# The second weight matrix of a dense layer: turned on TensorE, or read and converted a second time

## The chip, the cores and the metric

One core of one Trainium2 chip runs the whole program. The metric is the device time of one execution in microseconds (us). The kernel before took 642.76 us, the median of three runs (639.36, 642.76 and 643.01).

## The reference: what is computed

Three stages follow one another.

```
attention, 4 batches x 12 heads, 448 tokens, head width 64:
  s = 30 * tanh(q k^T / 8 / 30);  x = softmax(s) v            -> x: 1792 tokens x 768
dense layer:  r = relu(x @ w_in);  g = s*r*r + b;  y = g @ w_out   w_in 768x2048, w_out 2048x768
soft mixture on y:  logits = y @ phi (32 slots)
  d = softmax over tokens, c = softmax over slots
  slot_in = d^T y;  h = relu(slot_in[e] @ w1[e]);  out = c @ (h @ w2[e])     8 experts, 4 slots each
```

The inputs are float32, but `w_in` and `w_out` arrive as float64 and have to be made into float32 on the chip. The program never forms y. It uses `w_out @ phi` (for the logits), and applies `w_out` once to the 32 rows of slot inputs, near the end. So it needs `w_out` with the 2048 hidden units on the partitions in the tail, and with the 768 output columns on the partitions for the product with `phi`.

## The kernel before

**Blocks.** One batch is one block (448 tokens), 0 to 3. `hidden` makes relu(x w_in)^2 of a block in 16 slices `fc` of 128 hidden units, each with 18 products `hp` (L527): six 128-row pieces of x times three products, since each fp32 factor is split in two parts, hi and lo. The attention of block b+1 is laid between the products of block b, so TensorE does both in blocks 0 to 2. Block 3 has no attention beside it. The tail applies `w_out`, `w1` and `w2` to the slots.

**Attention.** Heads go in fours (`Q`, twelve in all, three to a block). `scores` (L137, L134) or, from the seventh four on, `visit` (L165, L155) makes a piece of 128 keys: products `sc` of 64 rows, two heads side by side in the array, three products per factor split. `weighted` (L243) makes `U`: products with 32 columns, four heads side by side. `sums` (L226) makes the softmax sums the same way, and `post` (L564) the logits `L`.

**Weights of a slice.** A slice's `w_in` arrives in `wr`; `w_split` makes each of its two halves into hi (ScalarE, L511) and lo (VectorE, L512) in `ws`. Three halves are held: two belong to the slice in work, one to the next. `wr` has three buffers.

**Conversion.** `convert` takes float64 pieces of 128 x 768 (768 KB, buffer `raw`, three of them). A piece costs one pass on ScalarE (L372) and three on VectorE (L377, L401, L405). The 16 pieces of `w_in` go into `wr` and, for blocks 1 to 3, to DRAM (`wsc`), from where L498 reads them again. `w_out` comes in transposed form (`w_outT`): 8 pairs of pieces into a buffer `o`, of which there is one. For a pair, `down` multiplies by `phi` (`pp`, L457), `fold` adds up (`pf`, L465), and three calls of `wturn` turn it by 128 x 128 transposes on TensorE (`tw`, L475, four a call), copy the result from PSUM (ScalarE, L477) and store it to DRAM (`osc`, L478). The tail reads `osc` in the wanted form. Turns, transposes of r (`tp`, L550), sums, `pp` and `pf` share one PSUM bank until block 3.

**Order.** Engines run their instructions in a fixed order each. A scheduler makes this order when the program is built: it takes what is ready by its own estimates, the earliest traced first, unless a priority or an issue-after edge says otherwise. `convert` is a generator that is advanced once per third of a slice in blocks 0 and 1 (`block`, L802), and when a slice of `w_in` or a part of `w_out @ phi` is needed. All loads and stores of weights are issued on one queue, SP's, in order. The program holds two copies of the body, chosen by a flag at run time; cap is 30 here, so the first runs.

Of the kernel before, what the change touches and what calls it, by code (L numbers as in the profile page):

```python
# [7 lines left out]
F32 = mybir.dt.float32  # L8
# [9 lines left out]
P = 128  # L18
B, H, S, D = 4, 12, 448, 64
# [4 lines left out]
DM = H * D  # L24
KC = DM // P
FF = 2048
FC = FF // P
# [6 lines left out]
KF = S // P  # L34
# [6 lines left out]
LAST = 3  # L41
CASTS = 8
LEAD = 10
WIDE = 6
VISITS = (4, 7, 10, 13)
U = 256
CU = 768
HOLD = 2
XPOS = (1, 4, 7, 10, 13, 15, 15, 15)
POSTS = [[(), (), (0,), (1,)], [(-2,), (-1,), (0, 1), (2,)], [(-1,), (0,), (1,), (2,)], [(-1,), (0,), (1,), (2,)]]  # L50
OUT_GROUPS = [(0, 4), (4, 6)]
# [8 lines left out]
class Body:  # L60
    def __init__(self, nc, tc, io, consts, general, f64, wsc, osc):
        self.nc, self.tc, self.io, self.c, self.general = nc, tc, io, consts, general
        self.f64, self.wsc, self.osc = f64, wsc, osc
        self.ws, self.wr = {}, {}
        self.x = {}
        self.qk = {}
        self.r2 = {}
        self.e = {}
        self.v = {}
        self.nslot = 0  # L70
        self.later, self.wide, self.nsplit = [], False, 0
        self.nx = 0
        self.mark = None
        self.raws = 3

    def bank(self, name):
        return self.pst[0].tile([P, 512], F32, tag="T", bufs=self.pst[1], name=name)
# [48 lines left out]
    def scores(self, p, c):  # L126

        nc = self.nc
        Q, j = divmod(p, 2)
        qh, ql, kh, kl = self.qk[p]  # L130
        sc = (self.ps2 if self.ps2 is not None and j else self.psa).tile([P, 2, 512], F32, tag="sc", bufs=1, name="sc")
        for n, (k, q) in enumerate(((kh, qh), (kh, ql), (kl, qh))):
            if c == KF:
                nc.tensor.matmul(sc[:, 0, :S], k[:, KF * P:], q, start=(n == 0), stop=(n == 2))  # L134
            for i in range(2) if c < KF else ():
                r = slice(64 * i, 64 * i + 64)
                nc.tensor.matmul(sc[:, i, :S], k[r, c * P:(c + 1) * P], q[r, :], start=(n == 0), stop=(n == 2))  # L137
        if j == 0:
            self.e.setdefault(Q, []).append(self.ap.tile([P, 4 if c < KF else 2, S], F32, tag="e", bufs=4 if self.general else 3, name="e"))
        if c < KF:  # L140
            nc.scalar.activation(self.e[Q][c][:, 2 * j:2 * j + 2, :], sc[:, :, :S], AF.Tanh, scale=self.c["tsc"])  # L141
        else:
            nc.scalar.activation(self.e[Q][c][:, j, :], sc[:, 0, :S], AF.Tanh, scale=self.c["tsc"])
        if c == NCH - 1:
            del self.qk[p]

    def visit(self, Q, c):

        nc = self.nc
        t = [self.qk[2 * Q + j] for j in range(2)]  # L150
        if c == KF:
            sc = self.psa.tile([P, 2, 512], F32, tag="sc", bufs=1, name="sc")
            for j, (qh, ql, kh, kl) in enumerate(t):
                for n, (k, q) in enumerate(((kh, qh), (kh, ql), (kl, qh))):
                    nc.tensor.matmul(sc[:, j, :S], k[:, KF * P:], q, start=(n == 0), stop=(n == 2))  # L155
            self.e[Q].append(self.ap.tile([P, 2, S], F32, tag="er", bufs=1, name="er"))
            nc.scalar.activation(self.e[Q][c], sc[:, :, :S], AF.Tanh, scale=self.c["tsc"])
            del self.qk[2 * Q], self.qk[2 * Q + 1]
            return
        sc = [self.psa.tile([P, 2, 512], F32, tag=n, bufs=1, name="sc") for n in ("sc", "U")]  # L160
        for j, (qh, ql, kh, kl) in enumerate(t):
            for n, (k, q) in enumerate(((kh, qh), (kh, ql), (kl, qh))):
                for i in range(2):
                    r = slice(64 * i, 64 * i + 64)
                    nc.tensor.matmul(sc[j][:, i, :S], k[r, c * P:(c + 1) * P], q[r, :], start=(n == 0), stop=(n == 2))  # L165
        self.e.setdefault(Q, []).append(self.ap.tile([P, 4, S], F32, tag="e", bufs=3, name="e"))
        for j in range(2):
            nc.scalar.activation(self.e[Q][c][:, 2 * j:2 * j + 2, :], sc[j][:, :, :S], AF.Tanh, scale=self.c["tsc"])  # L168
# [65 lines left out]
    def weighted(self, Q, chunks):  # L234

        nc = self.nc
        if chunks[0] == 0:
            self.U = self.psa.tile([P, 2, 512], F32, tag="U", bufs=1, name="U")
        for k in chunks:
            for h in range(2):  # L240
                for i in range(4):
                    d = (i % 2 * KF + k if k < KF else 2 * KF) * D + 32 * h
                    nc.tensor.matmul(self.U[32 * i:32 * i + 32, h, :S], self.v[2 * Q + i // 2][self.rows(i, k), d:d + 32], self.chunk(4 * Q + i, k),  # L243
                                     start=(k == 0), stop=(k == KF))

    def finish(self, Q):

# [176 lines left out]
    def conv_units(self):  # L424


        nc, io, c = self.nc, self.io, self.c
        cur = {}
# [9 lines left out]
        def across(fh, half):  # L438
            if half == 0:
                self.wide = True  # L440
                cur["o", fh] = self.cv.tile([P, KC * U], F32, tag="o", bufs=1, name="o")
            return cur["o", fh][:, half * CU:(half + 1) * CU]

        def proj(fh, half):
            if half == 0:
                return
            o = cur.pop(("o", fh)).rearrange("p (a b) -> p a b", b=U)
            self.later = [lambda: down(fh, o)]
            if self.f64:
                self.later += [lambda th=th: wturn(fh, th, o) for th in range(3)]  # L450
            self.later.insert(2, lambda: fold(fh))

        def down(fh, o):
            pp = self.bank("pp")
            for kc in reversed(range(KC)):
                j = kc % 4
                nc.tensor.matmul(pp[32 * j:32 * j + 32, :U], c["phi"][:, kc, :], o[:, kc, :], start=(kc + 4 >= KC), stop=(kc < 4))  # L457
            nc.scalar.copy(c["tmp"][:, S + U * (fh % 2):S + U * (fh % 2 + 1)], pp[:, :U])
            self.wide = self.f64

        def fold(fh):
            ps = c["tmp"][:, S + U * (fh % 2):S + U * (fh % 2 + 1)]
# [5 lines left out]
            if self.nx == FF // U:  # L468
                self.bias()

        def wturn(fh, th, o):
            tw = self.bank("tw")
            for j in range(2):
                for k in range(2):
                    nc.tensor.transpose(tw[:, (2 * j + k) * P:(2 * j + k + 1) * P], o[:, 2 * th + k, j * P:(j + 1) * P], c["idn"])  # L475
            n = o[:, 2 * th:2 * th + 2, :].rearrange("p a b -> p (a b)")
            nc.scalar.copy(n, tw)  # L477
            nc.sync.dma_start(self.osc[th][:, 2 * U * fh:2 * U * (fh + 1)], n)  # L478
            self.wide = th < 2

        units = []
        for fc in range(FC):
            units.append((io["w_in"][fc], lambda fc=fc: place(fc), lambda o, fc=fc: keep(fc, o), lambda fc=fc: self.nsplit + 3 > fc))
            for fh in range(FF // U):
                if XPOS[fh] == fc:
                    units += [(io["w_outT"][fh, h], lambda fh=fh, h=h: across(fh, h), lambda o, fh=fh, h=h: proj(fh, h), lambda h=h: h or not self.wide) for h in range(2)]
        return units

    def w_need(self, i):
# [228 lines left out]
    def prefetch(self, upto, behind=False):  # L718

        while self.nslot < min(upto, 54):  # L720
            k, h = divmod(self.nslot, 2)
            self.wt[k, h] = self.half(self.nslot)
            src = (self.osc if self.f64 else self.io["w_out"])[k] if k < 3 else self.io["w1"][k - 3] if k < 15 else self.io["w2"][k - 15]
            with self.tc.issue_after(self.mark) if behind else nullcontext():
                self.nc.sync.dma_start(self.wt[k, h], src[:, 2048 * h:2048 * (h + 1)])
            self.nslot += 1
# [59 lines left out]
    def block(self, bi, atn):  # L786
# [5 lines left out]
        for grp in range(4):  # L792
# [6 lines left out]
            for k in range(12):  # L799
                next(h)  # L800
                next(post, None)
                if bi < 2:  # L802
                    next(self.conv, None)
                while done < min(total, (12 * grp + k + 1) * total / (48 - LEAD)):
                    next(atn)
                    done += 1
# [122 lines left out]
def tile_kernel(ctx: ExitStack, tc: tile.TileContext, io):  # L929
# [43 lines left out]
    t("pb", [P, 1])  # L973
    t("ct", [P, NT], F32R)
    f64 = io["w_in"].dtype == I64
    osc = []
    dp = ctx.enter_context(tc.tile_pool(name="dp", bufs=1, space=DRAM))
    wsc = [dp.tile([P, KC * P], F32, name=f"wsc{i}") for i in range(FC)]
    if f64:
        osc = [dp.tile([P, 4096], F32, name=f"osc{i}") for i in range(3)]  # L980
    rv = nc.values_load(flag, min_val=0, max_val=1, skip_runtime_bounds_check_because="a comparison writes 0 or 1")
    with tc.If(rv > 0) as br:
        Body(nc, tc, io, c, False, f64, wsc, osc).run()
# [4 lines left out]
def layouts(inputs):  # L988
# [19 lines left out]
    wi = wi.reshape(NQ, 4, 2, D // 2, FF).transpose(0, 2, 1, 3, 4)  # L1008
    a["w_in"] = cc(wi.reshape(KC, P, FC, P).transpose(2, 1, 0, 3)).reshape(FC, P, KC * P)
    a["w_outT"] = cc(wo.reshape(FF // U, U, 2, KC // 2, P).transpose(0, 2, 4, 3, 1)).reshape(FF // U, 2, P, CU)  # L1010
    if not f64:
        a["w_out"] = cc(wo.reshape(FC, P, 3, U).transpose(2, 1, 0, 3)).reshape(3, P, 4096)
    a["phi"] = cc(inputs["moe2_phi"].reshape(KC, P, NS).transpose(1, 0, 2))
    a["w1"] = cc(inputs["moe2_w1"].reshape(2, 4, KC, P, F2).transpose(0, 2, 3, 1, 4)).reshape(2 * KC, P, 4096)
    a["w2"] = cc(inputs["moe2_w2"].reshape(2, 4, FC2, P, NPC, P).transpose(4, 0, 3, 2, 1, 5)).reshape(2 * NPC, P, 4096)
# [32 lines left out]
```

## Time and profile before

| | |
|---|---|
| runs | 639.36, 642.76, 643.01 us |
| profiled execution | 638.93 us, span of its instructions 637.2 us |
| TensorE (PE) busy, weight loads (PEld) | 593.7 us, 396.3 us |
| VectorE (DVE), ScalarE (ACT) busy | 343.4 us, 402.1 us |
| HBM read, written | 118.49 MB, 18.09 MB |
| first `hp` of blocks 0, 1, 2, 3; last `hp` | 66.5, 196.6, 327.9, 446.6; 523.9 us |

A row of the page or of the trace gives an engine, a line of the kernel, the tile written and the tiles read. A fp32 product that is not split appears as two records, so `U` of a four of heads, one piece of keys, is 16 records. Matmuls overlap: the next starts while one is still under way. So the time that a group takes from TensorE is read from its first start to the first start of the next group, not from the length of its records.

### The profile page before, as it was taken

What the parts mean: (1) busy time and instruction counts of PE and PEld (TensorE: products, weight loads), DVE (VectorE), ACT (ScalarE), POOL (GpSimd) and SP (SyncE); (2) the same over time, 40 slices, a digit from 0 to 9 for tenths busy, and PEclk for the clock granted to TensorE, in tenths of its full rate; (3) what the DMA queues carried; (4) which work ended last, traced back from release to release, by engine and by line L of the source; (5) the groups of instructions that cost most, each with busy time, mean ns of one, the idle gap of its engine ahead of it and who ended that gap; (6) DMA issues with size and microseconds to landing.
All of it is one profiled execution on the core that took longest, in us unless ns stands there. A gap on an engine that the chain in (4) does not pass through costs nothing.

```text
span 637.2 us, 11290 instructions
## 1 busy us (share of the span) xinstructions
PE 593.7 (93%) x4592; PEld 396.3 (62%) x4592; DVE 343.4 (54%) x509; ACT 402.1 (63%) x683; POOL 4.1 (1%) x11
## 2 busy tenths in 40 slices
PE   8898999999999999999999999999999998998672
PEld 5333575746776747567687476768868884346461
DVE  4998899878894482844624825454332224112121
ACT  5887889879867959679569386866645662001010
POOL 1000000000000000000000000000000000000000
PEclk9998999999999999999999999999999999999997
DMA  8843778786685442221421221211968859999998
GB/s 297 290 128 115 269 262 300 252 274 199 235 299 198 136 154 83 87 78 50 141 75 52 84 75 40 72 54 56 394 256 313 315 190 394 421 419 417 419 412 318
DMA packets 39626, 137.38 MB, mean 216 GB/s; under 512 B 4352, under 2 KB 12304, under 8 KB 32656
## 3 DMA queue, kind: packets, MB, share of 16 engines
q1 hardware_dynamic: 39280, 136.07, 59.2%
q8 instruction: 38, 0.62, 0.4%
q0 software_dynamic: 288, 0.53, 0.2%
q14 instruction: 20, 0.16, 0.1%
HBM read 118.49 MB, written 18.09 MB: 214 GB/s over the span
## 4 chain that ended last, share of the span: by engine, by line
PE 65%; DMA 14%; DVE 9%; ACT 8%; issue 3%; SPq 0%; DVEq 0%; ACTq 0%
PE hp L527 32%; DMA wt<-in_w_dram 12%; PE U L243 9%; PE tp L550 4%; PE sc L165 3%; PE pt L640 2%; PE L L564 2%; PE sc L137 2%; PE Sm L226 2%; ACT e L206 2%; ACT e L168 1%; PE tw L475 1%; DVE rec L232 1%; DMA osc<-o 1%; PE pp L457 1%
## 5 line engine op out<-in xcount | busy, mean ns | idle before, releaser
L527 PE MATMUL hp<-x,ws 128*128 128x448 f32 x1152 | 271.4, 376 | 0.0
L527 PEld LDWEIGHTS hp<-x,ws 128*128 128x128 f32 x1152 | 206.4, 188 | 42.2 <-issue 29.4
L512 DVE TENSOR_TENSOR ws<-wr,ws 128x384 fp32r<-128x384 f32 x128 | 70.6, 553 | 123.3 <-ACT ws L511 123.1
L511 ACT CAST ws<-wr 128x384 fp32r<-128x384 f32 x128 | 66.8, 524 | 36.8 <-PE hp L527 36.3
L243 PE MATMUL U<-e,v 128*32 128x448 f32 (+1 forms) x672 | 75.8, 551 | 4.7 <-ACT e L206 3.7
L206 ACT ACTIVATE e<-e,c_acap 128x1792 f32<-128x1792 f32 (+1 forms) x42 | 71.5, 1702 | 0.5
L552 ACT COPY g<-tp 112x256 f32<-112x256 f32 x128 | 43.3, 385 | 12.8 <-PE tp L550 12.0
L243 PEld LDWEIGHTS U<-e,v 128*32 128x32 f32 (+1 forms) x672 | 20.7, 110 | 45.4 <-issue 36.3
L232 DVE RECIPROCAL rec<-rec 128x448 f32<-128x448 f32 x12 | 35.4, 2950 | 18.1 <-ACT rec L231 18.1
L141 ACT ACTIVATE e<-sc,c_tsc 128x896 f32<-128x896 f32 x36 | 35.9, 1008 | 12.9 <-PE sc L137 11.9
L533 ACT ACTIVATE r<-hp 128x448 f32<-128x448 f32 x63 | 34.9, 554 | 9.8 <-PE hp L527 9.8
L550 PE MATMUL tp<-c_cst,r 128*112 128x128 f32 x256 | 39.0, 275 | 1.7 <-ACT g L552 1.4
L897 ACT COPY wt<-op 128x512 f32<-128x512 f32 x12 | 7.0, 586 | 50.6 <-PE op L892 50.6
L168 ACT ACTIVATE e<-sc,c_tsc 128x896 f32<-128x896 f32 x36 | 36.1, 1035 | 4.0 <-PE sc L165 4.0
L534 ACT ACTIVATE r<-r 128x448 f32<-128x448 f32 x63 | 37.6, 596 | 0.4
L912 PE MATMUL so_ps<-wt,free 128*32 128x128 f32 x768 | 26.5, 282 | 10.9 <-DMA wt<-in_w_dram 10.5
L550 PEld LDWEIGHTS tp<-c_cst,r 128*112 128x112 f32 x256 | 29.5, 133 | 11.3 <-ACT g L552 3.8
L215 DVE TENSOR_TENSOR es<-e 128x1792 f32<-128x1792 f32 x12 | 24.3, 2022 | 13.7 <-ACT e L206 13.7
L912 PEld LDWEIGHTS so_ps<-wt,free 128*32 128x32 f32 x768 | 20.8, 113 | 15.2 <-DMA wt<-in_w_dram 12.8
L215 DVE TENSOR_TENSOR es<-es,e 128x1792 f32<-128x1792 f32 x12 | 24.3, 2022 | 9.6 <-ACT e L206 9.6
L231 ACT ACTIVATE rec<-Sm,c_eps 128x448 f32<-128x448 f32 x12 | 7.7, 638 | 28.9 <-PE Sm L226 28.9
L863 PE MATMUL hps<-wt,free 128*32 128x512 f32 x192 | 21.0, 593 | 0.0
(186 smaller groups left out, 705.9 us busy)
## 6 DMA issues: line engine op xcount, KB each, us to landing
wt<-in_w_dram SPq DMA_DIRECT2D x48, 1024.0 KB, 16.5
wr<-wsc SPq DMA_DIRECT2D x48, 384.0 KB, 3.1
raw<-in_w_in_dram SPq DMA_DIRECT2D x16, 768.0 KB, 5.2
raw<-in_w_outT_dram SPq DMA_DIRECT2D x16, 768.0 KB, 5.8
wsc<-wr SPq DMA_DIRECT2D x16, 384.0 KB, 3.0
osc<-o SPq DMA_DIRECT2D x24, 256.0 KB, 2.9
wt<-osc SPq DMA_DIRECT2D x6, 1024.0 KB, 7.0
k<-in_kT_dram SPq DMA_DIRECT2D x22, 256.0 KB, 3.4
```

What stands on the lines that cost most here:

```text
L168: nc.scalar.activation(self.e[Q][c][:, 2 * j:2 * j + 2, :], sc[j][:, :, :S], AF.Tanh, scale=self.c["tsc"])
L206: ins = self.nc.scalar.activation(e, e, AF.Exp, scale=self.c["acap"]).ins
L215: self.nc.vector.tensor_add(es, e[0] if c == 1 else es, e[c])
L232: nc.vector.reciprocal(self.rec, self.rec)
L243: nc.tensor.matmul(self.U[32 * i:32 * i + 32, h, :S], self.v[2 * Q + i // 2][self.rows(i, k), d:d + 32], self.chunk(4 * Q + i, k), start=( ...
L511: self.nc.scalar.copy(hi, u)
L512: self.nc.vector.tensor_sub(lo, u, hi.bitcast(F32))
L527: nc.tensor.matmul(hp[:, :S], ws[kc // 3][:, w, kc % 3, :], x[:, s, kc, :], start=(k == 0), stop=(k == 3 * KC - 1))
L534: self.mark = nc.scalar.activation(r2, r2, AF.Square).ins
L550: self.nc.tensor.transpose(tp[:CP, q * P:(q + 1) * P], r2[:, q * CP:(q + 1) * CP], self.c["idn"])
L552: self.nc.scalar.copy(self.g[q][:CP, :, fc * P:(fc + 1) * P], tp[:CP, 2 * q * P:2 * (q + 1) * P].rearrange("p (a b) -> p a b", b=P))
L912: nc.tensor.matmul(so_ps[32 * e:32 * e + 32, G, :], ht[G][:, f, 32 * e:32 * e + 32], w2[f // 4][:, f % 4, e, :], start=(f == 0), stop=(f = ...
```

## The change

`wturn` is gone: no transposes `tw`, no copies from PSUM, no stores of turned pieces. Instead `w_out` is given to the program a second time, untransposed, in 16 pieces of 768 KB. They are units of the same generator `convert`, behind all others, and they may start when slices 22, 23, 25, 26, 28, ... 44 (of 64, counted over the blocks) have been split: in blocks 1 and 2. Each is stored to `osc` as three runs of 1 KB per partition. The generator is now advanced in all blocks, and holds four turns instead of two before it does `down`. The second part is `together`: the products of a score visit, or of a call of `weighted`, are placed behind their first one with a high priority (for `weighted` from the fourth four of heads on, for scores from the third pair on). In `visit` the hi and lo parts now come in the opposite order.

```diff
+VISIT = 3000
+LAY = (22, 3, 2)
-HOLD = 2
+HOLD = 4
...
+    def together(self, products, near=True):
+
+        if not near:
+            products = [f() for f in products]
+            return
+        first, rest = products[0](), products[1:]
+        with self.tc.issue_after(first.ins), self.tc.high_priority(VISIT):
+            for p in rest:
+                p()
...
+        if p < 2:
+            for f in products:
+                f()
+        else:
+            self.together(products)
...
+        self.together([lambda j=j, n=n, k=k, q=q, i=i, r=r: nc.tensor.matmul(sc[j][:, i, :S], k[r, c * P:(c + 1) * P], q[r, :], start=(n == 0), stop=(n == 2))
+                       for j, (qh, ql, kh, kl) in enumerate(t) for n, (k, q) in enumerate(((kl, qh), (kh, ql), (kh, qh))) for i, r in enumerate(half)])
...
+        self.together(products, Q >= 3)
...
-            self.later = [lambda: down(fh, o)]
-            if self.f64:
-                self.later += [lambda th=th: wturn(fh, th, o) for th in range(3)]
-            self.later.insert(2, lambda: fold(fh))
+            self.later = [lambda: down(fh, o), lambda: fold(fh)]
...
-            self.wide = self.f64
+            self.wide = False
...
-        def wturn(fh, th, o):
-            tw = self.bank("tw")
-            for j in range(2):
-                for k in range(2):
-                    nc.tensor.transpose(tw[:, (2 * j + k) * P:(2 * j + k + 1) * P], o[:, 2 * th + k, j * P:(j + 1) * P], c["idn"])
-            n = o[:, 2 * th:2 * th + 2, :].rearrange("p a b -> p (a b)")
-            nc.scalar.copy(n, tw)
-            nc.sync.dma_start(self.osc[th][:, 2 * U * fh:2 * U * (fh + 1)], n)
-            self.wide = th < 2
+        def lay(fc):
+            if fc % 2 == 0:
+                cur["n"] = self.cv.tile([P, KC * U], F32, tag="o", bufs=1, name="o")
+            return cur["n"][:, fc % 2 * DM:(fc % 2 + 1) * DM]
+
+        def store(fc, o):
+            nc.sync.dma_start(self.osc.rearrange("p (t f d) -> p t f d", t=3, d=U)[:, :, fc, :], o.rearrange("p (t d) -> p t d", d=U))
...
+        a, n, d = LAY
+        for fc in range(FC if self.f64 else 0):
+            units.append((io["w_out"][fc], lambda fc=fc: lay(fc), lambda o, fc=fc: store(fc, o), lambda fc=fc: self.nsplit >= a + fc * n // d))
...
-                if bi < 2:
-                    next(self.conv, None)
+                next(self.conv, None)
...
-        osc = [dp.tile([P, 4096], F32, name=f"osc{i}") for i in range(3)]
+        osc = dp.tile([P, 3 * 4096], F32, name="osc")
```

TensorE's order in block 0, a little past its middle, before: a score visit (three rows `sc`, two products each) and a `U` of 16 products.

```order
L137 MATMUL sc<-qh,kh 128x448 x2
L243 MATMUL U<-e,v 32x448 x5
L137 MATMUL sc<-ql,kh 128x448 x2
L457 MATMUL pp<-o,c_misc 32x256 x6
L137 MATMUL sc<-qh,kl 128x448 x2
L243 MATMUL U<-e,v 32x448 x4
L475 MATMUL tw<-c_cst,o 128x128 x4
L243 MATMUL U<-e,v 32x448 x7
L527 MATMUL hp<-x_398,ws 128x448 x6
```

The same place in the order of the change:

```order
L146 MATMUL sc<-qh,kh 128x448 x2
L146 MATMUL sc<-ql,kh 128x448 x2
L146 MATMUL sc<-qh,kl 128x448 x2
L257 MATMUL U<-e,v 32x448 x16
L238 MATMUL Sm<-es,c_ones 32x448 x4
L541 MATMUL hp<-x_396,ws 128x448 x6
L564 MATMUL tp<-c_cst,r_794 112x128 x4
```

The visit and `U` stand in one piece each and `tw` is gone. Between the first and the last `hp` of the program, runs of `sc` go from 65 (28, 21 and 16 in blocks 0, 1 and 2) to 49 (22, 14, 13), runs of `U` from 17 (10, 3, 4) to 12 (6, 3, 3), and runs of `tw` from 24 (18, 6, 0) to none.

VectorE's order in the second half of block 2, before: the last step of a four of heads (`U` times the reciprocal of the sums, then the lo part of x) and the lo parts of the weights, `ws`.

```order
L255 TENSOR_TENSOR U<-U,rec 128x2x448
L512 TENSOR_TENSOR ws<-wr,ws 128x384
L81 TENSOR_TENSOR x_2321<-U,x_2321 128x896
L512 TENSOR_TENSOR ws<-wr,ws 128x384 x9
L215 TENSOR_TENSOR es<-e 128x1792
```

In the order of the change, the same step and what follows it:

```order
L271 TENSOR_TENSOR U<-U,rec 128x2x448
L526 TENSOR_TENSOR ws<-wr,ws 128x384
L421 SCALAR_TENSOR_TENSOR o<-raw,o 128x768
L93 TENSOR_TENSOR x_2168<-U,x_2168 128x896
L526 TENSOR_TENSOR ws<-wr,ws 128x384 x3
L393 TENSOR_SCALAR o<-o 128x768
L526 TENSOR_TENSOR ws<-wr,ws 128x384
L417 SCALAR_TENSOR_TENSOR o<-raw,o 128x768
L393 TENSOR_SCALAR o<-o 128x768
L421 SCALAR_TENSOR_TENSOR o<-raw,o 128x768
L526 TENSOR_TENSOR ws<-wr,ws 128x384
L417 SCALAR_TENSOR_TENSOR o<-raw,o 128x768
```

Passes of the second conversion (`o`) now stand between the `ws` rows, up to three in a row.

## Rows read from the trace of the kernel before

**Rows 1.** The page, part 1: busy time of each engine and its share.
```profile
PE 593.7 (93%) x4592; PEld 396.3 (62%) x4592; DVE 343.4 (54%) x509; ACT 402.1 (63%) x683; POOL 4.1 (1%) x11
```
**Rows 2.** Busy by stretch: blocks 0 to 3, tail; us, PE, PEld, DVE, ACT, POOL, clock, DMA.
```profile
66.50:196.60 130.10, 128.53 (x825) 85.32 (x824) 112.33 (x141) 107.68 (x176) 0.00 (x0) 1.00 0.77 265
196.60:327.90 131.30, 128.72 (x868) 87.15 (x867) 71.85 (x100) 97.88 (x173) 0.54 (x1) 1.00 0.34 107
327.90:446.60 118.70, 117.74 (x778) 81.67 (x777) 58.07 (x76) 84.59 (x146) 0.00 (x0) 1.00 0.21 63
446.60:524.50 77.90, 77.90 (x448) 64.36 (x447) 22.50 (x49) 45.49 (x108) 0.00 (x0) 1.00 0.77 292
524.50:637.20 112.70, 83.04 (x1264) 51.17 (x1262) 24.67 (x66) 13.80 (x27) 0.54 (x1) 0.94 0.99 400
```
**Rows 3.** PE's waits in block 0: us in total, times, longest.
```profile
PE pp L457 <- DVE o L405: 1.0, 2, 0.8
```
**Rows 4.** PE's waits in block 1.
```profile
PE pp L457 <- DVE o L405: 1.8, 2, 1.4
```
**Rows 5.** Timeline of PE, a turn between other products: start, length, what.
```profile
173.00 0.66 PE L475 MATMUL tw<-c_cst,o 128*128 128x128 f32 x4
173.41 0.85 PE L527 MATMUL hp<-x,ws 128*128 128x448 f32 x3
```
**Rows 6.** Timeline of PE in block 0, a visit and a U in pieces.
```profile
132.44 0.48 PE L137 MATMUL sc<-qh,kh 64*128 64x448 f32 x2
132.85 1.69 PE L243 MATMUL U<-e,v 128*32 128x448 f32 x10
134.47 0.47 PE L137 MATMUL sc<-ql,kh 64*128 64x448 f32 x2
134.87 1.06 PE L457 MATMUL pp<-o,c_misc 128*32 128x256 f32 x12
135.86 0.47 PE L137 MATMUL sc<-qh,kl 64*128 64x448 f32 x2
136.26 1.82 PE L243 MATMUL U<-e,v 128*32 128x448 f32 x8
138.01 0.66 PE L475 MATMUL tw<-c_cst,o 128*128 128x128 f32 x4
138.60 1.70 PE L243 MATMUL U<-e,v 64*32 64x448 f32 x14
140.23 1.48 PE L527 MATMUL hp<-x,ws 128*128 128x448 f32 x6
```
**Rows 7.** Timeline of PE in block 0, a visit and a U in one piece.
```profile
76.09 0.48 PE L137 MATMUL sc<-qh,kh 64*128 64x448 f32 x2
...
76.91 3.21 PE L243 MATMUL U<-e,v 128*32 128x448 f32 x32
80.05 1.27 PE L527 MATMUL hp<-x,ws 128*128 128x448 f32 x5
```
**Rows 8.** DVE and others from 78 to 110 us, columns as in Rows 2.
```profile
78.00:110.00 32.00, 30.87 (x210) 20.40 (x204) 31.14 (x40) 29.20 (x45) 0.00 (x0) 1.00 0.79 282
```
**Rows 9.** Groups by line, whole span: busy us, mean ns, idle before.
```profile
L401 DVE SCALAR_TENSOR_TENSOR o<-raw,o 128x768 int32<-128x768 int32 x16 | 15.1, 951 | 0.1
L405 DVE SCALAR_TENSOR_TENSOR o<-raw,o 128x768 int32<-128x768 int32 x16 | 15.1, 950 | 0.1
L372 ACT ACTIVATE o<-raw 128x768 f32<-128x768 f32 x16 | 14.4, 929 | 1.8 <-DMA osc<-o 1.1 <-DMA raw<-in_w_outT_dram 0.7
L477 ACT COPY o<-tw 128x512 f32<-128x512 f32 x24 | 14.1, 586 | 5.8 <-PE tw L475 5.7
L377 DVE TENSOR_SCALAR o<-o 128x768 int32<-128x768 int32 x16 | 8.8, 554 | 3.2 <-ACT o L372 3.1
```
**Rows 10.** Groups of DVE by line within block 0 alone.
```profile
L405 DVE SCALAR_TENSOR_TENSOR wr<-raw,wr 128x768 int32<-128x768 int32 x13 | 12.3, 950 | 0.1
L405 DVE SCALAR_TENSOR_TENSOR o<-raw,o 128x768 int32<-128x768 int32 x10 | 9.5, 950 | 0.0
```

More of the change, by code (lines that the diff above doesn't have):

```diff
@@ L131, in scores @@
         sc = (self.ps2 if self.ps2 is not None and j else self.psa).tile([P, 2, 512], F32, tag="sc", bufs=1, name="sc")
[L132 to L137, printed above, removed]
+        halves = [(0, slice(0, P))] if c == KF else [(i, slice(64 * i, 64 * i + 64)) for i in range(2)]
+        terms = ((kh, qh), (kh, ql), (kl, qh))
+        products = [lambda n=n, k=k, q=q, i=i, r=r: nc.tensor.matmul(sc[:, i, :S], k[r, c * P:(c + 1) * P], q[r, :], start=(n == 0), stop=(n == 2))
+                    for n, (k, q) in enumerate(terms) for i, r in halves]
+        if p < 2:
[3 more added lines that the diff above has]
+            self.together(products)
         if j == 0:
@@ L152, in visit @@
             sc = self.psa.tile([P, 2, 512], F32, tag="sc", bufs=1, name="sc")
-            for j, (qh, ql, kh, kl) in enumerate(t):
-                for n, (k, q) in enumerate(((kh, qh), (kh, ql), (kl, qh))):
-                    nc.tensor.matmul(sc[:, j, :S], k[:, KF * P:], q, start=(n == 0), stop=(n == 2))
+            self.together([lambda j=j, n=n, k=k, q=q: nc.tensor.matmul(sc[:, j, :S], k[:, KF * P:], q, start=(n == 0), stop=(n == 2))
+                           for j, (qh, ql, kh, kl) in reversed(list(enumerate(t))) for n, (k, q) in enumerate(((kl, qh), (kh, ql), (kh, qh)))])
             self.e[Q].append(self.ap.tile([P, 2, S], F32, tag="er", bufs=1, name="er"))
@@ L160, in visit @@
         sc = [self.psa.tile([P, 2, 512], F32, tag=n, bufs=1, name="sc") for n in ("sc", "U")]
[L161 to L165, printed above, removed]
+        half = [slice(64 * i, 64 * i + 64) for i in range(2)]
+        self.together([lambda j=j, n=n, k=k, q=q, i=i, r=r: nc.tensor.matmul(sc[j][:, i, :S], k[r, c * P:(c + 1) * P], q[r, :], start=(n == 0), stop=(n == 2))
+                       for j, (qh, ql, kh, kl) in enumerate(t) for n, (k, q) in enumerate(((kl, qh), (kh, ql), (kh, qh))) for i, r in enumerate(half)])
         self.e.setdefault(Q, []).append(self.ap.tile([P, 4, S], F32, tag="e", bufs=3, name="e"))
@@ L238, in weighted @@
             self.U = self.psa.tile([P, 2, 512], F32, tag="U", bufs=1, name="U")
-        for k in chunks:
+        order = tuple(chunks)
+        products = []
+        for k in order:
             for h in range(2):
@@ L242, in weighted @@
                     d = (i % 2 * KF + k if k < KF else 2 * KF) * D + 32 * h
-                    nc.tensor.matmul(self.U[32 * i:32 * i + 32, h, :S], self.v[2 * Q + i // 2][self.rows(i, k), d:d + 32], self.chunk(4 * Q + i, k),
-                                     start=(k == 0), stop=(k == KF))
+                    products.append(lambda k=k, h=h, i=i, d=d: nc.tensor.matmul(
+                        self.U[32 * i:32 * i + 32, h, :S], self.v[2 * Q + i // 2][self.rows(i, k), d:d + 32], self.chunk(4 * Q + i, k),
+                        start=(k == 0), stop=(k == KF)))
+        self.together(products, Q >= 3)
     def finish(self, Q):
@@ L722, in prefetch @@
             self.wt[k, h] = self.half(self.nslot)
-            src = (self.osc if self.f64 else self.io["w_out"])[k] if k < 3 else self.io["w1"][k - 3] if k < 15 else self.io["w2"][k - 15]
+            src = (self.osc[:, 4096 * k:4096 * (k + 1)] if self.f64 else self.io["w_out"][k]) if k < 3 else self.io["w1"][k - 3] if k < 15 else self.io["w2"][k - 15]
             with self.tc.issue_after(self.mark) if behind else nullcontext():
@@ L975, in tile_kernel @@
     f64 = io["w_in"].dtype == I64
-    osc = []
+    osc = None
     dp = ctx.enter_context(tc.tile_pool(name="dp", bufs=1, space=DRAM))
@@ L1010, in layouts @@
     a["w_outT"] = cc(wo.reshape(FF // U, U, 2, KC // 2, P).transpose(0, 2, 4, 3, 1)).reshape(FF // U, 2, P, CU)
-    if not f64:
-        a["w_out"] = cc(wo.reshape(FC, P, 3, U).transpose(2, 1, 0, 3)).reshape(3, P, 4096)
+    a["w_out"] = wo.reshape(FC, P, DM) if f64 else cc(wo.reshape(FC, P, 3, U).transpose(2, 1, 0, 3)).reshape(3, P, 4096)
     a["phi"] = cc(inputs["moe2_phi"].reshape(KC, P, NS).transpose(1, 0, 2))
```

## The prediction

> **What bounds the kernel now.** I read first the page's busy times [rows 1]: TensorE is busy 93% of the span, ScalarE 63%, VectorE 54%. A mean over stages decides nothing, so next the stretches of the four blocks and the tail [rows 2]. In blocks 0 to 3 TensorE is busy 128.5 of 130.1, 128.7 of 131.3, 117.7 of 118.7 and 77.9 of 77.9 us, at the full granted clock. Blocks 1 and 2 leave VectorE 59.5 and 60.6 us idle, and ScalarE 33.4 and 34.1. Block 0 is different: VectorE is busy 112.3 of 130.1 us (86%) and ScalarE 107.7 (83%). The tail moves 400 GB/s at a DMA share of 0.99: its length is that of its loads. Those loads begin with block 3, so what the blocks gain shifts the tail as a whole, and no gain comes from it. Third, TensorE's waits: the longest in blocks 0 and 1 are for the last conversion pass before `pp`, 1.0 and 1.8 us in all [rows 3, 4]. So in the blocks time is the length of TensorE's own list, and I cost the change there first.
>
> **The turns go.** In the timeline a `tw` starts at 173.00 and the next product at 173.41 [rows 5]: 0.41 us for four transposes. 24 groups are removed, 18 in block 0 (7.4 us) and 6 in block 1 (2.5 us). With them go 24 copies on ScalarE at 0.586 us, 14.1 us [rows 9], which nobody on the path waits for, and 24 stores.
>
> **Groups are kept whole.** A visit and a `U` can stand in three pieces each [rows 6]. The visit's pieces last 0.41, 0.40 and 0.40 us to the next start, together 1.21; in one piece it takes 76.91 - 76.09 = 0.82 [rows 7]. So an extra piece costs (1.21 - 0.82) / 2 = 0.20 us. The pieces of `U` last 1.62, 1.75 and 1.63, together 5.00, against 80.05 - 76.91 = 3.14 for the same 32 records: 0.93 us an extra piece. The two orders give 6, 7 and 3 fewer visit pieces in blocks 0, 1 and 2, so 1.2, 1.4 and 0.6 us; and 4, 0 and 1 fewer pieces of `U`, so 3.7, 0 and 0.9. What a piece costs the product in front of it is not counted, and would add to the gain.
>
> TensorE's list gets shorter by 12.3 us in block 0 (7.4 + 1.2 + 3.7), 3.9 in block 1 and 1.5 in block 2, in all 17.7.
>
> **What holds block 0.** VectorE loses nothing there: `tw` had no work on it, and the second conversion comes later. Its 112.3 us would stand in 130.1 - 12.3 = 117.8, a share of 95%. Between 78 and 110 us it reaches 31.14 of 32.00, 97% [rows 8], and TensorE is busy 30.87 there, so such a share is possible; over the block it has 86%. At 97% block 0 could take 115.4 us and nothing is given back; at 86% it stays at 130.1 and all 12.3 are. I take 92%, between the two and nearer to the stretch where this limit already shows: 122.1 us, and 4.3 us given back.
>
> **What is added.** 16 conversions. On ScalarE 16 x 0.929 = 14.9 us, some 11 more in blocks 1 and 2 than the six copies that leave block 1, into 67 us of idle time: no cost. On VectorE each takes 0.554 + 0.951 + 0.950 = 2.46 us [rows 9], in all 39.3, into 120 us of idle time in blocks 1 and 2 [rows 2]. That idle time is the cover; without it the cost is 39.3. But the queue is strict: a `ws` half behind a pass comes later, and `hp` reads it. The order shows at most three passes in a row, 2.46 us, while TensorE has two more halves, each nine products. The nearest row is block 0: 23 conversions were ended there (13 of `w_in`, 10 of `w_out`) [rows 10], and TensorE's wait for VectorE was 1.0 us. Bounds 0 and 39.3; I take 1.0.
>
> Small edits together. 16 loads of 768 KB are 12.6 MB, some 50 GB/s more in blocks 1 and 2, where 107 and 63 flow [rows 2]: covered. They stand on SP's queue with the loads of `wr`, which are ahead by two slices; a load that waits for its `raw` buffer holds `wr` back by what the conversion is late, so this is the same cover. A store in 384 runs of 1 KB has no row. It could only be felt through the single buffer `o`, for which ScalarE waited 1.1 us in all before [rows 9]; eight more such pairs cost ScalarE as much again, off the path. The last store stands nine weight loads ahead of the tail's first load of `osc`, so that is in time. Holding four turns instead of two lets the last pass end before `pp`: of the 2.8 us of waits [rows 3, 4] all could go or as much again could come, since TensorE is now ahead; I take 0. The reversed order of parts in a visit has its latest operand first and costs nothing.
>
> **The sum.** 17.7 - 4.3 - 1.0 = 12.4 us. The profiled execution took 638.93 us, at the low end of the runs (639.36 to 643.01, median 642.76); 12.4 off it is 626.5. The four times before have a mean of 641.0, 2.1 above the profiled one, and I expect the median after to lie as far above: **628 us**.
>
> **The rivals.**
>
> *VectorE holds block 0 (chance 0.18).* If its idle 17.8 us there are all dependencies that move with it, the block stays at 130.1, and only 3.9 + 1.5 - 1.0 = 4.4 us are gained: 636.6 us as a median. For it speaks the 97% stretch, against it that VectorE's stretches outside are looser and TensorE hardly ever waited for it. The Trainium skill (Perfetto Trace Analysis, Identifying the Most-Contended Engine) says that busy time of matmuls is no good measure, that one should go by the weight loads, and that the engine with the highest share is the one to work on. By that rule TensorE in block 0 is at 85.3 / 130.1 = 66%, behind VectorE, and cutting its list would give this rival's time. The trace agrees for the busy share, which counts overlap; but starts follow one another without a gap [rows 6, 7], which no share of weight loads shows, so I keep it at this chance.
>
> *Nothing is given back (0.20).* VectorE goes to 97%: all 17.7 us count, 638.9 - 17.7 + 2.1 = 623 us, and some 3 us less if pieces cost their predecessors 0.1 us each or the waits for `pp` [rows 3, 4] go too.
>
> *The kept groups do not pay (0.06).* A product that used to fill a wait of a visit is now barred by the priority, so TensorE waits inside the group. Only the turns then count, less what block 0 gives back, 9.9 - 4.3 - 1.0 = 4.6, and waits of some 0.1 us in each of 49 visits take that: about 641 us. Against it: the orders put a group where all its operands are traced well before.
>
> *Slower: the second conversion stands in the way (0.07).* If each conversion delays a `ws` half beyond the two that TensorE still has (18 products at some 0.2 us with what lies between), its 2.46 us come onto the path: 638.9 - 17.7 + 39.3 + 2.1 = 662.6 us. It decides once more than half of the conversions are exposed (over 17 to 24 us). Against it is block 0, denser and without such waits; for it, that the scheduler's estimates place them, not the chip.
>
> **How the numbers follow.** Forecast 0.49, the rivals 0.18, 0.20, 0.06 and 0.07. The likeliest is 628. The forecast with its bounds runs from 622 to 633; the range takes in the full gain (620 to 623, down to 617 when the runs fall as low as the profiled one did) and VectorE's hold (637, up to 640 by the spread of the runs): 617 to 640. Left out are most of the slower case and of the groups that do not pay. A measurement of this kernel tells 1% from no change: below 636.3 is faster. That holds the forecast, the full gain and half of VectorE's hold: 0.78. Within 1%: the other half, the groups and a part of the slower case: 0.16. Slower: 0.06.
>
> **What would show it.** In the profile after: no `tw`; a visit of six products at 0.82 us and a `U` of 32 records at 3.14 everywhere; block 0 at 122 us with VectorE near 112 busy in it; blocks 1 and 2 at some 128 and 118, with VectorE some 20 us a block busier and no wait of `hp` for `ws`; the tail at 112.7 us as before. The prediction is wrong if block 0 stays near 130, if `hp` waits for `ws` by more than a few us, if TensorE waits inside groups, or if the tail grows by what the blocks lose.

## The result and the profile after

The change takes 623.69 us, the median of four runs (623.18 to 626.88), against 641.77 before (the three runs above and one more, 639.36 to 643.01). The ratio is 0.9731, interval 0.9697 to 0.9766: 2.7% faster. It lies inside the forecast range, 4.3 us below the 628 us. The profiled execution took 623.18 us, with a span of 621.3.

First the stretches of the profile after, with the columns of the table before: prelude, blocks 0 to 3, tail.

```profile
0.00:63.80 63.80, 55.48 (x419) 25.51 (x419) 54.08 (x78) 52.93 (x56) 2.99 (x9) 0.97 0.63 215
63.80:183.60 119.80, 116.67 (x753) 77.97 (x751) 111.98 (x142) 99.34 (x160) 0.00 (x0) 1.00 0.73 251
183.60:310.60 127.00, 124.52 (x843) 84.31 (x842) 95.86 (x136) 101.17 (x176) 0.54 (x1) 1.00 0.62 208
310.60:428.70 118.10, 116.32 (x777) 81.34 (x777) 67.20 (x89) 87.67 (x150) 0.00 (x0) 1.00 0.33 101
428.70:506.60 77.90, 77.90 (x448) 64.39 (x448) 22.52 (x49) 45.48 (x108) 0.00 (x0) 1.00 0.78 291
506.60:621.30 114.70, 82.13 (x1264) 50.19 (x1262) 24.69 (x66) 13.87 (x27) 0.54 (x1) 0.96 0.97 394
```

Read against [rows 2]: block 0 fell from 130.1 to 119.8 us, block 1 from 131.3 to 127.0, block 2 from 118.7 to 118.1. Block 3 is the same. The prelude (all before the first `hp`) fell from 66.5 to 63.8 and the tail rose from 112.7 to 114.7, neither of which I had forecast. Together these are the 15.9 us between the two spans. TensorE is busy 11.9 us less in block 0, and VectorE has the same work there in a shorter time: 111.98 of 119.80 us, 93%. In blocks 1 and 2 VectorE is busy 24.0 and 9.1 us more, where I had expected some 20 in each.

The timeline of TensorE in block 0 after the change answers to [rows 6]: a visit, one product `hp`, and a `U`, each in one piece.

```profile
105.37 0.47 PE L146 MATMUL sc<-qh,kh 64*128 64x448 f32 x2
105.68 0.36 PE L146 MATMUL sc<-ql,kh 64*128 64x448 f32 x2
105.89 0.36 PE L146 MATMUL sc<-qh,kl 64*128 64x448 f32 x2
106.18 0.47 PE L541 MATMUL hp<-x,ws 128*128 128x448 f32 x1
106.58 3.21 PE L257 MATMUL U<-e,v 128*32 128x448 f32 x32
109.61 1.03 PE L470 MATMUL pp<-o,c_misc 128*32 128x256 f32 x12
```

The visit takes 106.18 - 105.37 = 0.81 us and the `U` 109.61 - 106.58 = 3.03, close to the whole ones of before (0.82 and 3.14) [rows 7]; no `tw` stands anywhere. What TensorE waits for in block 0 (us in total, times, longest) is small:

```profile
PE pp L470 <- ACT r L547: 1.8, 1, 1.8
PE sc L146 <- ACT e L156: 1.3, 2, 1.0
```

Visits wait for the `tanh` that empties their banks. The first row names ScalarE, but the wait of `pp` for the last conversion pass [rows 3] is not gone. These are the rows of ScalarE, VectorE and TensorE that lead to that `pp`:

```profile
173.86 0.89 ACT L388 ACTIVATE o<-raw 128x768 f32<-128x768 f32 x1 [3.47 <-DMA raw<-in_w_outT_dram]
178.06 0.95 DVE L421 SCALAR_TENSOR_TENSOR o<-raw,o 128x768 int32<-128x768 int32 x1
179.16 1.06 PE L470 MATMUL pp<-o,c_misc 128*32 128x256 f32 x12 [1.82 <-ACT r L547]
```

The last pass on `o`, which `pp` reads, ends at 179.01 on VectorE, and `r` at 179.08 on ScalarE: even without `r`, `pp` could have started no more than 0.1 us sooner. The chain goes back to a load of `raw` that is issued at 166.19 and lands at 173.84, for which ScalarE is idle 3.47 us. The two further profiles of this kernel, e0 and e8, show the same chain. In blocks 1 and 2 no `hp` waits for `ws`; the longest wait there is 0.9 us.

### The profile page after: what moved, and what is told of

Read it like the earlier page. It is cut to its first block, busy times and chain, and to the rows that moved or that the text cites. A ratio compares the mean times of both kernels' runs of the same rounds, so it can differ in the third digit from the quotient of the medians.

```text
span 621.3 us, 11132 instructions
## 1 busy us (share of the span) xinstructions
PE 573.0 (92%) x4496; PEld 383.7 (62%) x4496; DVE 376.3 (61%) x557; ACT 400.4 (64%) x675; POOL 4.1 (1%) x11
## 4 chain that ended last, share of the span: by engine, by line
PE 59%; DMA 14%; ACT 13%; DVE 9%; issue 3%; SPq 0%; DVEq 0%; ACTq 0%
PE hp L541 30%; DMA wt<-in_w_dram 12%; PE U L257 9%; PE tp L564 4%; ACT e L218 3%; ACT e L180 3%; PE sc L146 2%; PE pt L654 2%; PE sc L176 2%; PE L L578 2%; PE Sm L238 2%; ACT e L156 1%; ACT g L566 1%; DMA raw<-in_w_outT_dram 1%; ACT ws L525 1%
## 5 line engine op out<-in xcount | busy, mean ns | idle before, releaser
L541 PE MATMUL hp<-x,ws 128*128 128x448 f32 x1152 | 267.6, 375 | 0.0
L257 PE MATMUL U<-e,v 128*32 128x448 f32 (+1 forms) x672 | 70.4, 548 | 3.3 <-ACT e L218 2.5
L566 ACT COPY g<-tp 112x256 f32<-112x256 f32 x128 | 44.2, 404 | 12.3 <-PE tp L564 11.5
L564 PE MATMUL tp<-c_cst,r 128*112 128x128 f32 x256 | 39.3, 275 | 3.2 <-ACT g L566 2.4
L388 ACT ACTIVATE o<-raw 128x768 f32<-128x768 f32 x32 | 29.9, 949 | 5.3 <-DMA raw<-in_w_outT_dram 3.7
L925 PEld LDWEIGHTS so_ps<-wt,free 128*32 128x32 f32 x768 | 19.9, 109 | 18.1 <-DMA wt<-in_w_dram 15.6
L417 DVE SCALAR_TENSOR_TENSOR o<-raw,o 128x768 int32<-128x768 int32 x32 | 30.5, 954 | 0.3
L421 DVE SCALAR_TENSOR_TENSOR o<-raw,o 128x768 int32<-128x768 int32 x32 | 30.4, 953 | 0.2
```

What stands on the lines that cost most here:

```text
L257: products.append(lambda k=k, h=h, i=i, d=d: nc.tensor.matmul(self.U[32 * i:32 * i + 32, h, :S], self.v[2 * Q + i // 2][self.rows(i, k), d ...
L541: nc.tensor.matmul(hp[:, :S], ws[kc // 3][:, w, kc % 3, :], x[:, s, kc, :], start=(k == 0), stop=(k == 3 * KC - 1))
L564: self.nc.tensor.transpose(tp[:CP, q * P:(q + 1) * P], r2[:, q * CP:(q + 1) * CP], self.c["idn"])
L566: self.nc.scalar.copy(self.g[q][:CP, :, fc * P:(fc + 1) * P], tp[:CP, 2 * q * P:2 * (q + 1) * P].rearrange("p (a b) -> p a b", b=P))
L925: nc.tensor.matmul(so_ps[32 * e:32 * e + 32, G, :], ht[G][:, f, 32 * e:32 * e + 32], w2[f // 4][:, f % 4, e, :], start=(f == 0), stop=(f = ...
```

## The experiments

Each is compared with runs of the kernel before on the same chip, taken beside it. The full change was run twice more, as e0 and e8. Spans of stretches are prelude, blocks 0, 1, 2, 3 and tail; each experiment has one profile.

**e0: the full change again.** No edit.

> The full change, on the chip of the other three runs, so that they are compared with it at the same place: 623.7 us, ratio to before 0.973; blocks 0, 1 and 2 at 119.8, 127.0 and 118.1 us, prelude 63.8, tail 114.7. If the tail is again 2 us longer than that of the kernel before, this is the change's; if it is at 113, it was this one execution's.

622.54 us, ratio 0.9707 (0.9652 to 0.9763). Stretches 65.1, 118.8, 129.7, 118.1, 77.9 and 113.1 us. The tail is at 113.1, near the 112.7 of before, and at 114.1 in e8. Over the profiles of all experiments it spreads as widely without a pattern, and e2, which keeps the turns, is 1.1 us above before. So the 2 us of the first profile are not shown to be the change's. The same holds for most of the gain in the prelude: it is 63.8 in one execution of this kernel and 65.1 in two. Block 1 spreads too: 127.0, 129.7, and 127.0 in e8; the 129.7 has a wait of 2.5 us before `ct_ps` that the first profile does not show.

**e1: the turns gone, no priority.**

```diff
     def together(self, products, near=True):
-        if not near:
+        if True:
             products = [f() for f in products]
             return
```

> The change without the priority: the turns are gone and w_out is converted a second time, but products of a visit and of U are placed as the scheduler likes. Its order has 62 runs of score products and 19 of U in blocks 0 to 2 (49 and 12 with the priority). My theory, that the blocks last as long as TensorE's list: 13 x 0.20 + 7 x 0.93 = 9.1 us above the full change, some 633 us, ratio to before 0.987; block 0 at 119.8 + 4 x 0.93 + 0.2 = 123.7 us. Rival, that VectorE holds block 0: its work there is the same as in the full change, so block 0 stays at 120 us and the total is near 628 us, ratio 0.979. Rival, that the kept groups do not pay: 624 us, as the full change.

631.16 us, ratio 0.9845 (0.9784 to 0.9907): 8.6 us above e0, which ran beside it, where I expected 9.1. The kept groups pay. But block 0 took 120.2 us, not 123.7, which is what the rival said. The stretch table of block 0, first of e1, then of e0:

```profile
65.60:185.80 120.20, 118.99 (x749) 78.01 (x748) 111.72 (x141) 98.77 (x158) 0.00 (x0) 1.00 0.71 246
```
```profile
65.10:183.90 118.80, 116.41 (x752) 78.06 (x751) 111.92 (x142) 99.48 (x160) 0.00 (x0) 1.00 0.72 250
```

The pieces cost TensorE 119.0 - 116.4 = 2.6 us of busy time in this block, not the 3.9 that I counted, and the full change loses half of that in waits: 2.4 us idle against 1.2. The `U` of the block take 23.0 us here, each counted to the next start, and 19.9 in e0, for five more pieces: 0.63 us a piece. They are cut by `pp` and `Sm`, which have 32 columns as `U` has; those of [rows 6] are cut by visits and `tw`. Most of what the priority gives shows in block 1, 133.5 us here, 129.7 in e0 and 127.0 in the first profile:

```profile
185.80:319.30 133.50, 129.29 (x848) 86.98 (x847) 94.43 (x131) 100.69 (x177) 0.54 (x1) 0.99 0.60 194
```

**e2: the kernel before with the priority.** `together` and the three functions that call it, with the opposite order of hi and lo parts in `visit`, put into the kernel before; turns and hold as they were.

```diff
+        self.together(products)        # in scores, from the third pair on
...
+        self.together(products, Q >= 3)        # in weighted
```

> The kernel before with the priority alone: the turns stay on TensorE, nothing is converted twice. Its order has 50 runs of score products, 13 of U and 25 of turns in blocks 0 to 2 (before: 65, 17 and 24). My theory: 15 x 0.20 + 4 x 0.93 = 6.7 us below before, some 635 us, ratio 0.9895, or 10 us above the full change; block 0 at 130.1 - 3.8 = 126.3 us. Rival, that VectorE holds block 0: block 0 at 128 us or above and a total of 638 us. Rival, that kept groups do not pay: 641 us, ratio 1.00.

632.78 us, ratio 0.9887 (0.9822 to 0.9952): 8.0 us below before (expected 6.7), 10.2 above e0 (expected 10). Block 0 took 125.2 us (expected 126.3). So the rivals in which kept groups do not pay, or VectorE holds the block at 128, are out.

The two halves add up as a whole: 9.6 us for the change without the priority (e1 against before), 8.0 for the priority, 18.2 for both (e0). In block 0 they do not: by the profiles e1 takes 9.9 us off it, e2 4.9 (1.2 of them turns that move into block 1), and both together 10.3 to 11.3. The traces show why in part: the visits of block 0 stand in 28 runs before, in 23 in e1, 23 in e2 and 22 after the change, so either half mends nearly all of them.

**e3: the second conversion without VectorE's passes.**

```diff
+    def times(self, n):
+        return (0, 0) if n >= 2 * FC else (1, 1)
...
+                for _ in range(self.times(n)[1]):
                     nc.vector.scalar_tensor_tensor(o, raw[n][:, :, 1], -0x80000000, o, ...)
```

> The full change without VectorE's three passes of the second conversion (39.3 us of VectorE in blocks 1 and 2); ScalarE's pass, the loads and the stores stay, so the tail works with w_out in a raw form. My theory, that these passes are hidden: 1 us below the full change at most, 622.7 to 624 us, ratio to before 0.972. Rival, that passes ahead of the lo parts of the weights, or ahead of sums, delay TensorE: 4 us or more below, 620 us or less, with the gain in blocks 1 and 2.

624.12 us, ratio 0.9729 (0.9668 to 0.9790), not below e0. VectorE's busy time in blocks 1 and 2 falls from 95.9 and 67.2 to 70.5 and 58.5 us, and the blocks take 129.9 and 119.2 (e0: 129.7 and 118.1). No cost of the passes shows; the intervals would let one of some 4 us pass. ScalarE's pass, the loads and the stores stay in this run, so it does not price them.

**e4 and e9: a hold of two turns.**

```diff
-HOLD = 4
+HOLD = 2
```

> The full change with the older hold of two turns before the product with phi. My theory, that the hold is worth nothing either way: 622.5 to 624 us, ratio to before 0.972, the wait before that product (1.5 to 1.8 us in block 0 of the full change) within 1 us of that. Rival, that the longer hold spares TensorE the wait for the last pass: 626 us or more, with new waits before that product in block 0.

> The full change with a hold of two turns, again, in five rounds. If the longer hold is worth what the first look showed (626.45 us, block 0 at 121.2 with waits before the product with phi and its fold): 3 to 4 us above the full change of this call, 626 us. If that was chance, as my forecast of no effect would have it: within 1 us of it.

626.45 us in e4, ratio 0.9774 (0.9733 to 0.9814); 624.89 us in e9, five rounds, ratio 0.9769 (0.9750 to 0.9788), where the full change beside it (e8) has 622.88 us and 0.9730 (0.9707 to 0.9752). The two intervals just touch; the medians differ by 2.0 us, and block 0 took 121.2 and 120.8 us in the two, against 118.8 to 119.8 in the three profiles with the hold of four. The waits of TensorE in block 0 of e9:

```profile
PE sc L146 <- ACT e L156: 2.0, 2, 1.7
PE pf L478 <- ACT c_tmp L471: 0.7, 1, 0.7
PE pp L470 <- DVE o L421: 0.3, 1, 0.3
PE Sm L238 <- DVE c_hh L479: 0.2, 1, 0.2
```

What follows the product with phi waits for its copy here, 0.7 us. But the waits add up to 3.2 us, against 3.1, 2.4 and 2.8 in the three profiles with the hold of four, so they do not explain the difference. Some 1 us of it is TensorE's own list: it is busy 117.4 us (117.6 in e4) against 116.4 to 116.7, and its `hp` stand in 42 runs instead of 37. So the longer hold is worth some 2 us by the medians, and the profiles point to the order it gives TensorE more than to waits it spares; I had forecast nothing.

**e5: the passes of the second conversion made twice.** As e3, with (2, 2) in place of (0, 0).

> The full change with each of VectorE's three passes of the second conversion made twice: 39.3 us more on VectorE in blocks 1 and 2, so that the tail's numbers change. VectorE is busy 95.9 of 129.7 and 67.2 of 118.1 us there, 84.7 us idle; with it 163 + 39 = 202 of 248 us, 82%. My theory, that the idle time is the cover: 0 to 3 us more, 622.5 to 626 us. Rival, that passes in front of the lo parts of the weights delay TensorE: half of the added time or more on the path, 640 us or above.

627.44 us, ratio 0.9799 (0.9762 to 0.9836). The full change did not run beside it; it is 4.6 us above e6, which did, and its gain on the kernel before is 13.1 us, where e0 has 18.2 and e8 16.5. That is 3 to 5 us of cost, a little more than I expected. Blocks 1 and 2 in the stretch table:

```profile
183.00:310.20 127.20, 124.04 (x843) 84.57 (x842) 104.93 (x148) 97.63 (x172) 0.54 (x1) 1.00 0.54 177
310.20:432.70 122.50, 117.98 (x777) 82.55 (x777) 93.16 (x125) 91.11 (x154) 0.00 (x0) 0.99 0.41 132
```

Block 1 is as short as in the full change with VectorE 82% busy; block 2, where more of the added passes fell, is 4.4 us longer. Of 39.3 us added to what is already there, 3 to 5 came onto the path. The cover holds for the passes of the change and starts to give at twice as many.

**e6: less work for VectorE in block 0.** In the first conversion of `w_out` two of three passes are left out.

```diff
+    def times(self, n):
+        return (1, 0) if n in (2, 3, 7, 8, 12, 13, 17, 18, 22, 23, 26, 27, 28, 29, 30, 31) else (1, 1)
```

> The full change without two of VectorE's three passes in the first conversion of w_out (0.951 us each, 20 of them in block 0, 8 in block 1), so that its last bits and signs are left out. VectorE has 19 us less in block 0, where it is busy 111.9 of 118.8 us. If VectorE holds block 0: the block falls to TensorE's busy time there, 116.4 us, or below, and the total to 619 to 620 us. If TensorE's list alone sets it: block 0 stays within 1 us of 119 and the total at 622.5 to 624.

622.88 us, ratio 0.9715 (0.9679 to 0.9751): no gain as a whole. Block 0:

```profile
63.50:181.10 117.60, 116.33 (x752) 78.00 (x751) 96.40 (x123) 99.37 (x160) 0.00 (x0) 1.00 0.75 259
```

VectorE is busy 15.5 us less than in e0, 82% of the block, and the block is 1.2 us shorter, while TensorE's busy time has not moved. The wait for `pp` at its end (1.8 us after the change, 1.5 in e0) is gone: the load of `raw` behind it is issued at 160.48 us in place of 166.19 and lands at 164.99, and the last pass ends at 166.56, 7.9 us ahead of `pp`. Both expectations missed a part: the block did not fall to 116.4 nor the total to 620, and the block fell by a little more than the 1 us that the second allowed. So VectorE's passes hold block 0 by one to two microseconds, mainly through that one `pp`. Not tried were an earlier load alone and less work for ScalarE, whose `tanh` makes the other waits. Block 1 took 130.9, with a wait before `ct_ps` as in e0.

**e7 and e10: the fifth pair of transposed `w_out` three slices later.**

```diff
-XPOS = (1, 4, 7, 10, 13, 15, 15, 15)
+XPOS = (1, 4, 7, 10, 15, 15, 15, 15)
```

> A version that may be better: the fifth of the eight pairs of transposed w_out is converted three slices later, so that two units (4.9 us of VectorE, 1.9 of ScalarE) leave block 0 for block 1, where VectorE is idle for 34 us. If VectorE holds block 0: one to two us less there, 621 us in all. If not, or if block 1 is held up by its first logits, which need that pair: 622.5 to 625 us.

> The full change with the fifth pair three slices later, again, in five rounds. If the first look holds (620.94 us, block 0 at 117.0 instead of 119, no wait before the product with phi at its end): 2 us below the full change of this call, 621 us. If not: the same as it.

620.94 us, ratio 0.9692 (0.9658 to 0.9727), and in five rounds 620.73 us, ratio 0.9716 (0.9694 to 0.9738), beside the full change's 0.9730. The median is some 2 us below the full change's in both, but in the five rounds the interval holds the change's ratio: not shown to be better. Its blocks 0 and 1 in e10:

```profile
63.80:180.80 117.00, 115.85 (x736) 77.12 (x735) 108.60 (x137) 97.61 (x157) 0.00 (x0) 1.00 0.72 245
180.80:309.20 128.40, 126.35 (x859) 85.20 (x858) 99.67 (x141) 103.36 (x179) 0.54 (x1) 1.00 0.65 217
```

Block 0 takes 117.0 us in both profiles and the `pp` that waited 1.8 us now stands in block 1.

**e8: the full change in five rounds.**

> The full change in five rounds, beside the next three on one chip: 622 to 624 us, ratio to before 0.972; block 0 at 119 us, block 1 at 127 to 130.

622.88 us, ratio 0.9730 (0.9707 to 0.9752). Stretches 65.1, 119.5, 127.0, 118.1, 77.9 and 114.1 us.

**e11: the second conversion started three slices later as well.**

```diff
-LAY = (22, 3, 2)
+LAY = (25, 4, 3)
```

> The version with the fifth pair later, and the second conversion started three slices later (slices 25 to 45 instead of 22 to 44), so that ScalarE and VectorE have less to do in block 1, where TensorE waits some 4 us for copies from the one PSUM bank, and more in block 2, where VectorE is idle for 51 us. If ScalarE's share of the second conversion holds block 1: 1 to 2 us below the version before it, 619 us. If the waits belong to the order of the sums and transposes: the same, 621 us. If the stores come late for the tail: 622 us or more, with a longer block 3 or tail.

622.11 us, ratio 0.9729 (0.9709 to 0.9749), not below e10. Block 1 took 130.0 us with ScalarE busy 103.2, as in e10: moving the start did not take work off ScalarE there, so whether its share holds block 1 stays open. The third case of the expectation, stores late for the tail, names this total, but block 3 is as long as in e10 and the tail is within the spread told at e0.

## Why the prediction was right, and where its sum was off

**TensorE's list bounds the blocks: right.** With every product counted to the next start and idle time left out, the list of block 0 goes from 128.9 us before to 116.7 in the first profile after and 116.4 in e0: shorter by 12.2 to 12.5, where the prediction has 12.3. Blocks 1 and 2 lose 3.9 to 4.1 and 1.5, for 3.9 and 1.5. Most of it came back as time. That the sum for block 0 fits so closely is partly luck: `tw` gives the 7.4 us that were counted, but the `U` give 2.2 for 3.7, the visits 2.1 for 1.2, the `hp` 1.4 to 1.7 that were not counted, and the sums take 1.1 more.

**The turns, 9.9 us: right on the list.** The `tw` of the kernel before hold TensorE for 7.35 us in block 0 and 2.36 in block 1, each counted to the next start. The 9.6 us of e1 against before and the 10.2 of e0 against e2 agree, but they hold the second conversion and the longer hold as well.

**Kept groups, 7.8 us: right in sum, not in place.** 8.0 and 8.6 us. In block 0, for which I counted 4.9, they are worth 3.7 us beside the turns (e2, without the turns that move) and 1.4 with the turns gone (e1 against e0): there most of the visits' pieces had gone with the turns, a piece of `U` costs 0.63 us, and part of the gain turns into waits. In block 1, for which I counted 1.4, e1 against e0 gives 3.8, while e2 is no shorter there than before.

**What block 0 gives back, 4.3 us: mis-sized.** This is the term that was off in size: "I take 92%, between the two". Block 0 fell by 10.3 to 11.3 us in three profiles, against a list shorter by 12.3: 1.0 to 2.0 us were given back, with VectorE at 93 to 94% in place of 92. They are TensorE's waits in the block, 1.2 us before and 2.4 to 3.1 after. e6 measures the same from the other side: 15.5 us less for VectorE bring 1.2. A share between 86% and 97% was the wrong question; VectorE was 86% busy because TensorE set the pace, and its share rose as far as the block shrank.

**The second conversion, 1.0 us: not told from nothing.** e3 shows no cost of its passes. The reason, idle time in blocks 1 and 2 and two more halves of `ws`, is borne out by e5, in which the double of it costs 3 to 5 of 39.3 us.

**The hold, 0: wrong in size.** It is worth some 2 us by the medians, inside the bounds of 2.8 either way, of which I took the middle. The waits it was aimed at [rows 3, 4] are not what it changed most: one of them is still there, and the profiles show about half of the gain in TensorE's list.

**The offset of 2.1 us** between a profiled run and the median was 0.5 here, which accounts for 1.6 of the 4.3 us between forecast and median. The 2.7 us of the prelude and the 2.0 of the tail, not forecast, nearly cancel.

The rivals: VectorE holding block 0 at 130 us did not happen, and with it falls what the Trainium skill (Perfetto Trace Analysis, Identifying the Most-Contended Engine) would have said of this block if TensorE is judged by its weight loads, one of the two measures that the section gives for it. VectorE had the highest share that way, yet taking 15.5 us from it in the changed kernel brought 1.2 us, and taking some 12.3 from TensorE, at 66% by weight loads, brought 10.3 to 11.3. "Nothing is given back", at 623 us, came nearest in number, by luck: 1 to 2 us were given back, and the hold returned as much. The groups pay (e2), and the second conversion does not stand in the way (e3). The opposite order of hi and lo parts in a visit, taken at no cost, was not tried by itself.

## What to carry to other kernels

Where an engine's starts follow one another without a gap, cost a change by start-to-start times on that engine's list, and take the busy share of the others as a result of its pace, not as a limit, until an experiment relieves them. Work that only rearranges data can be bought back with a second load and conversion, if the engines that convert have idle time in a later stage and hold buffers ahead. Keep products that run side by side in one piece: here what broke them up cost some 8 us, nearly as much as the turns.

## What the runs showed of the hardware

A `U` of 32 records cut in pieces by visits and `tw` costs 0.93 us an extra piece in one example [rows 6, 7], a visit 0.20. Where `pp` and `Sm`, of 32 columns like `U`, cut it (e1, block 0), an extra piece costs 0.63 us on average, and TensorE is busy 2.6 us more over the whole block; whether it matters what cuts a `U` stays open. Four 128 x 128 transposes hold TensorE for 0.41 us [rows 5]. The same kernel's prelude took 63.8, 65.1 and 65.1 us, its tail 114.7, 113.1 and 114.1 us: two executions differ by 1 to 2 us in stretches that no edit touched.
